# Linear attention times SwiGLU on one core: query weights prepared in other buffers, the denominators of half two placed later, phi of Q read from PSUM

## The chip, the cores and the metric

The kernel runs on one core of one Trainium2 chip. The metric is device microseconds of one execution, from the first to the last instruction of the core and what lies around them. A figure for a kernel is the median of several runs.

## The reference

The input is x, 2048 rows of 1024 in bf16. A layernorm without weights gives xn, and two branches read it.

```python
xn  = layernorm(x)                               # 2048 x 1024
q, k, v = split(xn @ wqkv)                       # 32 heads of 32
phi = lambda t: where(t > 0, t + 1, exp(t)) + 1e-6
kv  = einsum("hsd,hse->hde", phi(k), v)          # one 32 x 32 matrix a head
z   = sum of phi(k) over s
o   = (phi(q) @ kv) / (phi(q) . z + 1e-6)
s   = o @ wo
g   = silu((silu(xn @ w_gate) * (xn @ w_up)) @ w_down)    # inner width 3584
out = x + s * g
```

## The kernel before, in words

**How the work is multiplied.** Every large product is cut into pairs of output blocks, and a pair is computed with a seven-product scheme (products named 1, 2, 3, 4, 5, 6, 7 in `Pair`, L722). It needs sums and differences of the operand blocks: `WF.combos` (L639) makes four of them for a block of weights, each an instruction on 128x1024, and `WF.inner` (L648) makes those of a second level inside products 1, 5 and, for gate and up, 3. `XF.outer` and `XF.inner` do the same for the activations. `Pair` gathers the products in PSUM banks, with copies on ScalarE (ACT) and additions on VectorE (DVE), and calls `evac` for each finished quarter; a quarter comes from PSUM three times in four (`kind` is "ps") and from SBUF once (`kind` is "sb").

**Stages.** First the layernorm, the transposes and K and V: sixteen row tiles, two by two (`kv_steps`, L1156), with phi of K in `kv_out` (L1056) and the sums of phi(K) times V gathered in three banks by `a_tile`. Then the Q stage: four pairs (`q_pair`, L1271: row half p 0, 1 by weight half s 0, 1), whose `evac` calls `phi_evac` (L1035) and leaves phi(Q) in SBUF at 132 KB and above. Into it fall `kv_end` (L1200, scales the 32x32 matrices by DVE), `kvt` (their transposes on TensorE), `m_build` (L1225, sixteen products with wo that go to a scratch tensor in HBM) and `den_run(0)` (L1278, the denominators of head half one). Then 28 gate/up pairs (`gu_pair`, numbered z = 0 to 27 in the loop at L1585), the product of the normalised phi(Q) with the matrix of `m_build` (`s_pair`), and the down projection (`d_pair`). `normalise` (L1305) multiplies phi(Q) by the reciprocals, in eight calls at z = N0 to N0+7, and writes it to HBM.

**phi_evac.** ACT writes Exp of the bank to a temporary e (`H1`, one of twelve 1 KB slots); DVE does min(e, 1) + eps (L1038). With `relu` set, ACT reads the bank a second time for Relu into a second temporary and DVE adds the two (L1043, shown under L482, the line of `tt`). Otherwise one DVE instruction does max(source, 0) + e (L1045). For Q the choice is `RQ` (L312): the Relu form for quarters from PSUM. For K it is `RK` (L313): the Relu form for column block 0.

**Weights.** `wload` (L1239) takes the next number k (0, 1 are the two halves of the Q weights, 2 to 15 the gate/up blocks 0 to 13, 16 to 19 phi(Q)), loads two times 512 KB into one of three raw buffers, and plans combos and inner sums into one of three `cmb` and one of two `inn` buffers. Raw buffers are W0 (80 KB), W0+8 and R2 (198 KB). During K and V the places W0+8 to W0+28 and W0+40 to W0+44 hold sums of the K/V weights (`KC`, L957), W0+32 to W0+40 hold row tiles of x, W0+44 to W0+50 normalised rows, W0+28 to W0+32 and W0+50 to W0+52 phi(K); W0 to W0+8 and R2 are unused. The combos of Q, of gate/up block 0 (`GC0`) and all sums of activations run on DVE, the other combos and the inner sums of gate/up on GpSimd (POOL).

**What sets the order.** The code doesn't issue instructions as it goes. `Plan.op` (L77) records each operation with what it must wait for; `Plan.schedule` (L125) then plays all engines with durations of its own, lets TensorE choose within a window of 20 operations, the other engines by due time (`dl`), and fixes each engine's order; `emit` (L261) writes the waits. A load with `asap` goes as soon as its buffer is free; one without gets an extra wait on the TensorE operation that lies LEAD = 12 us ahead of its due time (L135). All DMAs go through SyncE's (SP's) queue. An operation that reads a PSUM bank is recorded as if it wrote it (L464), so readers of one bank follow one another, each with a wait, on the same engine too.

## Time and profile before

| | us |
|---|---|
| median of 5 runs | 748.19 |
| lowest, highest of them | 745.16, 751.69 |
| the profiled execution | 750.69 |
| its span on the core | 749.0 |
| TensorE busy in it | 712.6 |
| DVE, ACT, POOL busy in it | 588.6, 380.2, 261.4 |

The profiled execution is 1.69 us longer than its span, and 2.50 us longer than the median. Busy times of TensorE (PE) count pipelined matmuls, so a busy PE is not always at its full rate; idle PE time is what the views of waits name. In the trace the K/V stage ends near 113 us, the last phi of Q near 201 us, and the gate/up pairs reach from there to about 560 us.

### The profile page before, as it was taken

What the parts mean: (1) busy time and instruction counts of PE and PEld (TensorE: products, weight loads), DVE (VectorE), ACT (ScalarE), POOL (GpSimd) and SP (SyncE); (2) the same over time, 40 slices, a digit from 0 to 9 for tenths busy, and PEclk for the clock granted to TensorE, in tenths of its full rate; (3) what the DMA queues carried; (4) which work ended last, traced back from release to release, by engine and by line L of the source; (5) the groups of instructions that cost most, each with busy time, mean ns of one, the idle gap of its engine ahead of it and who ended that gap; (6) DMA issues with size and microseconds to landing.
All of it is one profiled execution on the core that took longest, in us unless ns stands there. A gap on an engine that the chain in (4) does not pass through costs nothing.

```text
span 749.0 us, 11806 instructions
## 1 busy us (share of the span) xinstructions
PE 712.6 (95%) x4247; PEld 399.6 (53%) x4247; DVE 588.6 (79%) x1127; ACT 380.2 (51%) x729; POOL 261.4 (35%) x230
## 2 busy tenths in 40 slices
PE   8998998887898899999999999999999999999996
PEld 3444444443565555556666666656554455464642
DVE  6998765999899889988888888889978965556433
ACT  4777755886646567665454454544664112121211
POOL 2011000245538547856678656712750000000000
PEclk9999999999999999999999999999999999999999
DMA  9834205131133464467322333235599257463622
GB/s 301 205 85 98 43 0 169 58 113 32 44 117 114 154 197 138 152 225 232 106 77 65 106 99 111 88 119 169 182 321 281 81 169 201 134 202 105 188 71 70
DMA packets 141978, 101.57 MB, mean 136 GB/s; under 512 B 19040, under 2 KB 137056, under 8 KB 141920
## 3 DMA queue, kind: packets, MB, share of 16 engines
q1 hardware_dynamic: 141920, 100.82, 44.8%
q8 instruction: 33, 0.54, 0.3%
q14 instruction: 25, 0.20, 0.1%
HBM read 68.16 MB, written 29.49 MB: 130 GB/s over the span
## 4 chain that ended last, share of the span: by engine, by line
PE 72%; DVE 13%; DMA 6%; ACT 5%; issue 3%; SPq 1%; DVEq 0%; ACTq 0%
PE ps L424 72%; DVE SB L482 8%; ACT SB L474 4%; DVE ps L482 1%; DMA out_dram<-SB 1%; DVE SB L1038 1%; DMA SB<-in_A_x_dram 1%; DMA SB<-SB 1%; DMA SB<-q_scratch 1%; DMA SB<-h_scratch 1%; ACT ps L474 1%; DVE SB L1045 1%; SPq L494 1%; DMA m_scratch<-SB 1%; DVE SB L1210 0%
## 5 line engine op out<-in xcount | busy, mean ns | idle before, releaser
L424 PE MATMUL ps<-SB 128*128 128x512 f16 (+4 forms) x4126 | 702.1, 331 | 24.8 <-DVE ps L482 9.0
L424 PEld LDWEIGHTS ps<-SB 128*128 128x128 f16 (+1 forms) x4126 | 393.8, 98 | 330.9 <-DVE ps L482 18.0
L482 POOL TENSOR_TENSOR SB<-SB 128x1024 f16<-128x1024 bf16 (+3 forms) x196 | 247.2, 1287 | 232.1 <-PE ps L424 112.3
L474 ACT ACTIVATE SB<-ps 128x256 f32<-128x256 f32 (+5 forms) x443 | 235.2, 566 | 143.3 <-PE ps L424 113.8
L482 DVE TENSOR_TENSOR SB<-SB 128x512 f16<-128x512 f16 (+11 forms) x360 | 238.2, 696 | 57.3 <-ACT SB L474 22.9
L482 DVE TENSOR_TENSOR SB<-ps,SB 128x256 f32<-128x256 f32 (+2 forms) x318 | 181.7, 592 | 54.8 <-PE ps L424 43.0
L482 DVE TENSOR_TENSOR ps<-ps,SB 128x512 f32<-128x512 f32 (+1 forms) x250 | 128.1, 527 | 26.0 <-PE ps L424 16.8
L474 ACT ACTIVATE ps<-ps 128x512 f32<-128x512 f32 (+1 forms) x172 | 84.4, 492 | 123.5 <-PE ps L424 91.2
L474 ACT ACTIVATE SB<-SB 128x512 f16<-128x512 f32 (+1 forms) x68 | 42.4, 624 | 88.0 <-DVE SB L482 87.9
L1002 POOL TENSOR_TENSOR rstd<-veps,neg_half 128x1 f32<-128x1 f32 x16 | 11.6, 733 | 65.1 <-DVE veps L1001 63.9
L1038 DVE TENSOR_SCALAR SB<-SB 128x512 f16<-128x512 f16 x64 | 24.4, 394 | 12.1 <-ACT SB L474 11.9
L474 ACT ACTIVATE SB<-SB,zc 128x512 bf16<-128x512 bf16 x32 | 22.3, 716 | 6.4 <-DVE SB L482 6.3
L474 ACT ACTIVATE SB<-SB,nmr,rstd 128x1024 f16<-128x1024 bf16 x12 | 14.6, 1234 | 1.1 <-DVE nmr L1004 1.1
L998 DVE BATCH_NORM_STATS2 stats<-SB 128x6 f32<-128x512 bf16 x16 | 11.0, 687 | 3.6 <-DMA SB<-in_A_x_dram 3.5
L1045 DVE SCALAR_TENSOR_TENSOR SB<-SB 128x512 bf16<-128x512 f32 x15 | 11.6, 781 | 0.1
L999 DVE BATCH_NORM_STATS2 stats<-SB 128x6 f32<-128x512 bf16 x16 | 10.9, 683 | 0.0
L424 PE MATMUL ps<-SB,ident 128*128 128x512 f16 x17 | 6.5, 557 | 1.4 <-POOL ident L505 1.4
L1045 DVE SCALAR_TENSOR_TENSOR SB<-ps,SB 128x512 bf16<-128x512 f32 x9 | 6.1, 685 | 0.0
L453 PE MATMUL ps<-ident,SB 128*128 128x128 f16 x40 | 3.1, 220 | 2.3 <-DVE SB L1210 1.4
L453 PEld LDWEIGHTS ps<-ident,SB 128*128 128x128 f16 x40 | 2.3, 98 | 4.9 <-DVE SB L1008 2.8
L424 PEld LDWEIGHTS ps<-SB,ident 128*128 128x128 f16 x17 | 2.1, 131 | 4.5 <-issue 2.8
L1295 DVE RECIPROCAL SB<-SB 128x64 f32<-128x64 f32 x8 | 4.3, 544 | 0.0
(28 smaller groups left out, 25.1 us busy)
## 6 DMA issues: line engine op xcount, KB each, us to landing
h_scratch<-SB SPq DMA_DIRECT2D x112, 128.0 KB, 2.0
SB<-h_scratch SPq DMA_DIRECT2D x16, 896.0 KB, 6.1
SB<-in_B_w_gate_dram SPq DMA_DIRECT2D x14, 512.0 KB, 4.2
SB<-in_B_w_up_dram SPq DMA_DIRECT2D x14, 512.0 KB, 5.3
SB<-in_B_w_down_dram SPq DMA_DIRECT2D x4, 1792.0 KB, 8.6
SB<-in_A_wqkv_dram SPq DMA_DIRECT2D x12, 512.0 KB, 8.4
SB<-in_A_x_dram SPq DMA_DIRECT2D x16, 256.0 KB, 4.7
SB<-r_scratch SPq DMA_DIRECT2D x32, 128.0 KB, 2.8
```

The lines of the kernel that those rows point to most:

```text
L424: last = h.matmul(o() if callable(o) else o, l() if callable(l) else l, r() if callable(r) else r, start=st, stop=sp, skip_group_check=True)
L453: last = h.transpose(o(), i(), ident[:, :])
L474: return op("act", reads, writes, lambda h: h.activation(ev(o), ev(i), func, **kw), n / 1200.0 + (0.055 if src == "ps" else 0.095) + (0.09 ...
L482: f = lambda h: h.tensor_tensor(ev(o), ev(a), ev(b), alu)
L494: f = lambda h: h.dma_start(ev(o), ev(i))
L998: dve([xr] + ([named("ve", 0)] if q == 1 else []), [sA], lambda h: h.bn_stats(stats[:, j, 0, :], xa[:, 0:512]), 512)
L999: dve([xr] + ([named("ve", 0)] if q == 1 else []), [sB], lambda h: h.bn_stats(stats[:, j, 1, :], xa[:, 512:1024]), 512)
L1002: pool([ver, nh_r], [rsr], lambda h: h.tensor_tensor(rstd[:, j, :], veps[:, j, :], neg_half[:, :], ALU.pow), 0.56)
L1038: dve([e], [e], lambda h: h.tensor_scalar(vap(e, FP16), vap(e, FP16), 1.0, EPS_PHI, ALU.min, ALU.add), 512, 3.84, urgent=PU).port = True
L1045: dve(reads + [e], [out_r], lambda h: h.scalar_tensor_tensor(out_ap, ev(src), 0.0, vap(e, FP16), ALU.max, ALU.add), 512, urgent=PU).port = ...
L1295: dve([ea], [ra], lambda h, q=q: h.reciprocal(vap(ra, F32)[:, q * 64:q * 64 + 64], vap(ea, F32)[:, q * 64:q * 64 + 64]), 400)
```

## The change

It has six parts. The raw buffers rotate in another order and from another start: Q weights half one goes to R2 and `cmb` at W0+32, half two to W0 and `cmb` at W0+16, gate/up block 0 to W0+8, block 1 to R2; from there on the rotation repeats every three blocks. The two Q loads lose `asap`; the second is due 20 us earlier (`QU`). Phi of Q always takes the L1045 form. `den_run(1)` is called at z = 2 in place of z = 0, `normalise` starts at z = 4 in place of 3, and the two early loads of down weights come at z = 13 in place of 12. A reader of a PSUM bank waits for earlier readers on other engines alone (`solo`). The buffers of the down projection (`HC`, `HT`, `H2`, `HI_AT`, `WI_AT`, the order in `cur`) move with the places that the last weight blocks leave free.

```diff
-    def op(self, eng, reads, writes, fn, busy, sem=None, ..., asap=False):
+    def op(self, eng, reads, writes, fn, busy, sem=None, ..., asap=False, solo=()):
...
+        for r in solo:
+            for k in r.keys:
+                preds.update(q for q in self.readers.get(k, ()) if q.eng != eng)
...
-                v.pool.pend.remove(o.idx)
+                v.pool.pend.remove(v.ops[0].idx)
...
-    RQ = lambda w, i, j, kind: kind == "ps"
+    RQ = lambda w, i, j, kind: False
-    N0, NA, WA = 3, 2, True
+    N0, NA, WA, QU, ZD = 4, 2, True, 20.0, 2
...
-            wr += [v.r for v in mine if v not in wv]
+            kw["solo"] = [v.r for v in mine if v not in wv]
...
-        raw_at = [W0 * KB, (W0 + 8) * KB, R2 * KB]
-        cmb_at = [(W0 + 16 + 8 * k) * KB for k in range(3)]
+        raw_at = [R2 * KB, W0 * KB, (W0 + 8) * KB]
+        cmb_at = [(W0 + 16 + 8 * k) * KB for k in (2, 0, 1)]
...
-            rk = (0, 1, 0)[k] if k < 3 else 2 - k % 3
+            rk = k % 3
...
-                        dsem("wr%d_%d_%d" % (rk, q, kts.start)), 512 * KB // len(src), asap=WA)
+                        dsem("wr%d_%d_%d" % (rk, q, kts.start)), 512 * KB // len(src), asap=WA and k > 1).urgent = QU if k == 1 else 0.0
...
-        HC = [80, 112, 199, 96, 87]
-        HT = [119, 122.5, 103, 106.5]
-        H2 = 103
+        HC = [88, 111, 199, 104, 80]
+        HT = [118, 121.5, 96.75, 100.25]
+        H2 = 96.75
...
-            if z == 0:
+            if z == ZD:
                 at.append(partial(den_run, 1))
...
-        cur, spare = [0, 2, 1, 3], 4
+        cur, spare = [0, 2, 3, 1], 4
```

## The prediction

> **What bounds the kernel now.** I read the page first, then busy time by stretch, then who TensorE (PE) waits for in the worst stretch.

> ```profile
> PE 712.6 (95%) x4247; PEld 399.6 (53%) x4247; DVE 588.6 (79%) x1127; ACT 380.2 (51%) x729; POOL 261.4 (35%) x230
> ```

> PE is the bound over the whole span, but not everywhere. Busy time by stretch (DMA share and clock at the end of each line):

> ```profile
> 80.00:100.00 20.00, 20.00 (x106) 9.51 (x105) 11.55 (x28) 14.38 (x26) 0.17 (x1) 1.00 0.14 27
> 100.00:113.00 13.00, 13.00 (x74) 6.39 (x73) 8.88 (x22) 7.61 (x15) 0.00 (x0) 1.00 0.00 0
> 113.00:203.00 90.00, 75.53 (x482) 41.07 (x484) 75.62 (x171) 64.20 (x132) 34.19 (x25) 0.98 0.28 85
> 340.00:380.00 40.00, 40.00 (x260) 25.32 (x259) 33.07 (x59) 21.30 (x43) 27.15 (x20) 1.00 0.44 138
> 177.70:181.10 3.40, 2.87 (x9) 1.31 (x10) 3.40 (x6) 1.09 (x2) 2.17 (x3) 0.50 0.00 0
> ```

> See that PE never idles at the end of K/V (80 to 113 us) and in the middle of gate/up (340 to 380), while the Q stage, 113 to 203, leaves it idle 90.00 - 75.53 = 14.5 us. DVE is as busy there as PE (75.62); ahead of it DVE is idle for 8.45 + 4.12 us. The last line is 3.4 us at half the clock. Who PE waits for from 112 to 220 us (us, times, longest):

> ```profile
> PE ps L424 <- DVE ps L482: 5.7, 4, 3.2
> PE ps L424 <- ACT ps L474: 3.1, 4, 1.0
> PE ps L424 <- ACT SB L474: 2.2, 2, 1.2
> PE ps L424 <- DVE SB L482: 1.6, 1, 1.6
> PE ps L453 <- DVE SB L1210: 1.4, 1, 1.4
> ```

> These 14.0 us are what the change can win. The longest wait, on the timeline:

> ```profile
> 170.66 5.34 DVE L1038 TENSOR_SCALAR SB<-SB 128x512 f16<-128x512 f16 x7
> 170.83 9.04 POOL L482 TENSOR_TENSOR SB<-SB 128x512 f16<-128x512 f16 x8 [0.87 <-DVE SB L482]
> 177.48 0.69 DVE L482 TENSOR_TENSOR ps<-ps,SB 128x512 f32<-128x512 f32 x1
> 178.23 3.72 PE L424 MATMUL ps<-SB 128*128 128x512 f16 x12 [3.19 <-DVE ps L482]
> ```

> Seven small DVE steps beside POOL's sums take 5.34 us, the bank addition behind them comes late, and PE idles 3.19 us. The DVE groups concerned, first in the Q stage, then in K/V (20 to 113 us), where POOL is nearly idle:

> ```profile
> L1038 DVE TENSOR_SCALAR SB<-SB 128x512 f16<-128x512 f16 x33 | 15.7, 499 | 2.8 <-ACT SB L474 2.8
> L482 DVE TENSOR_TENSOR SB<-SB 128x512 bf16<-128x512 f16 x25 | 11.4, 494 | 0.0
> L1045 DVE SCALAR_TENSOR_TENSOR SB<-SB 128x512 bf16<-128x512 f32 x8 | 6.8, 862 | 0.0
> ```

> ```profile
> L1038 DVE TENSOR_SCALAR SB<-SB 128x512 f16<-128x512 f16 x27 | 7.6, 284 | 9.2 <-ACT SB L474 9.2
> L482 DVE TENSOR_TENSOR SB<-SB 128x512 bf16<-128x512 f16 x14 | 5.6, 421 | 1.2 <-ACT SB L474 1.2
> L1045 DVE SCALAR_TENSOR_TENSOR SB<-ps,SB 128x512 bf16<-128x512 f32 x8 | 5.4, 685 | 0.0
> ```

> [...]L1038 has a mean of 499 ns beside POOL and 284 without, and additions on PSUM (128x512, one SBUF input) keep 696 and 688 ns in the Q stage. [...]the trace has 3.4 us at 0.50 right after the 3.19 us wait.[...]

> **The change part by part**, against the profiled execution of 750.69 us (span 749.0 and 1.7 around it).

> *Q weights earlier.* Half two's loads are issued at 116 and 122 us, its four combos (0.68 us each) and eight inner sums (0.29 each) follow from 126 us on DVE: 5.1 us of durations, 4.0 from start to start (instructions overlap by some 0.08). In the change they can run when K's last sums are used, by the places in the code about 105 us. Half one's, now at 107 to 113 us, can run once the last x tiles are normalised, before 90 us. That much DVE work finds 4.1 us idle in 100 to 113 and 8.45 in 80 to 100, where PE waits for nothing: I cost it at nothing. Without that cover (DVE late at the turn to Q) it costs up to 2. In the Q stage it frees DVE while `kv_end` runs: three combos (1.8 us) lie between 126.4 and 129.2, ahead of the eight L1210 steps for which the transposes wait 1.45. **-1.4**.

> *Loads.* In the trace of before, SP issues the Q half one loads at 13.0 and 14.6 us and those of gate/up block 1 at 18.0 and 24.1; these four leave the busy start (DMA share 0.94 in 0 to 20 us). PE's waits there come before 20 us and are on DVE and POOL, so nothing is won; bounds -0.5 to 0. The Q loads must instead be in time without `asap`: SP issues nothing between 84 and 113 us, so four issues of 0.4 us delay no one. Half two's leave 116 to 122, with only wo beside them.

> *Gate/up blocks 0 and 1 swap places.* Block 0 no longer waits for Q half one's raw buffer (loads at 149.6 and 156.1) but for V's sums, gone at about 125; its DVE combos (four of 0.68) and POOL's inner sums can start some 15 us earlier. Block 1 waits for Q half one instead, so POOL's four combos (2.2 us each, now 139.6 to 157.3) come after 160. POOL does the same work in another order[...]. It costs PE 1.57 us now at 158.4 (two L1038 in 2.57 us) and the 3.19 at 178.2. Bounds: both waits stay, or both go. I take half: **-0.8** and, with half of the slow clock's 3.4 x 0.5 = 1.7, **-2.4**.

> *Phi of Q.* 32 quarters, 24 from PSUM. ACT loses 24 Relu of 0.59 to 0.64 us, from start to start 0.48: 11.5 of its 64.2 us. DVE exchanges 24 additions (0.421) for 24 L1045 (0.685): 24 x 0.264 = +6.3 us. Each of the 24 also gives up one H1 slot. PE's ACT waits: 1.05 at 140.5 (ACT itself waited 1.12 for an m_scratch store to free its slot), 0.86 at 142.0, and behind both engines 0.54 at 150.9 and 1.17 at 185.2. I take nearly all of the first two and a third of the others: **-0.9, -0.7, -0.6**. DVE after: 75.6 - 4.0 + 6.3 = 77.9 us[...]. The 6.3 us lie beside PE unless DVE is last, as it is for 5.7 + 1.6 of PE's 14.0 us of waits; bounds 0 and 6.3; I take a third, **+2.1**. The bank is now held until DVE's last step, not ACT's: queued behind are the matmuls that reuse it.

> *Denominators of half two.* PE waits 1.59 us at 202.8 for the last phi before `den_run(1)`; 32 matmuls take 1.1. Two pairs later nothing waits: **-1.5**. The step's DVE part (0.42 + four of 0.54 = 2.6 us), its ACT copy and eight stores (SP, 0.6 each, 5 us) move from 204-214 to about 230. Behind them on SP stand h_scratch stores, whose slots are twelve, and loads that are early: 0, bound +1. `normalise` and two down loads come one pair (13 us) later; 203 to 350 us has the same DVE work (133 of 147), the down loads are due by their own time: 0, bounds -1 and +1.

> *solo.* Same-engine readers lose a wait. ACT's pairs are already interleaved (starts 0.27 to 0.5 us apart at 114.8 to 115.8): 0, bound -1. *Down buffers:* the same sizes in the places freed at the same times: 0, bound ±1.

> Sum: -1.4 - 0.8 - 2.4 - 0.9 - 0.7 - 0.6 + 2.1 - 1.5 = **-6.2**. Profiled: 744.5. The median of the runs shown is 2.5 below the profiled execution: 748.2 - 6.2 = **742.0**. Next late will be DVE in the Q stage.

> **Rivals.** *DVE keeps its waits (no change):* its 14.4 us of idle time in the Q stage come from the back and forth with PE, so they stay, and the stage lasts 77.9 + 14.4 = 92.3 us, +2.3; with -1.5 of the denominators +0.8: **749.0**. For it: DVE is already as busy as PE. Against: 5.3 us of the waits (3.1 + 2.2) are ACT's, and ACT is relieved. *Banks held by DVE (slower):* when DVE runs behind, as from 170.7 to 180.3, up to six banks of eight wait for L1045, which before ACT released. If PE loses 2.5 us more at each of the four turns between pairs, +10, less the kv_end, H1 and denominator gains of 3.8: +6.2, **754.4**.[...] *Nearly all waits go (more gain):* 14.0 + 1.7 less the 2.3 at 120.5, 125.3 and 195.0 us that no part touches: -13.4, **734.8**. *The Q loads come late,* since they have lost `asap`: half one's were issued 100 us ahead of their use, and LEAD is 12; a 512 KB load of wqkv takes 8.4 us (median), so they should be in time; if not, PE idles 2 to 5 us at 113 and the gain is gone: counted with no change.

> **How the numbers follow.** Forecast (-3.7 to -10) 0.58, more gain 0.12, no change 0.18, slower 0.12. Half a per cent, 3.7 us, is about what can be told from none. Faster is 0.58 + 0.12 = 0.70. The range runs from just above the large gain, 735.5, to 750, which takes in no change with its costs of +1 and leaves the slower case out; the forecast alone spans 738 to 744.5.

> **What would show it.** Right: no PE wait on L1210 near 130; combos of both Q halves before 113; block 0's POOL sums before block 1's; ACT near 52 us in the Q stage; den_run's matmuls near 230 with no wait; the stage some 6 us shorter, DVE above 90% busy. Wrong: PE waits on L1045 by name, waits for a Q load near 113, a second Exp/Silu table load, or new waits beyond 340 us.

## The result and the profile after

| | before | after |
|---|---|---|
| median, us | 748.32 (40 runs) | 744.71 (21 runs) |
| lowest, highest | 745.16, 752.60 | 742.46, 746.98 |
| profiled execution, span | 750.69, 749.0 | 742.46, 740.9 |

The ratio is 0.9947 (95%: 0.9935 to 0.9959): 3.6 us less by the medians, where 6.2 were forecast. The two profiled executions lie 8.2 us apart, because before's is one of its longer runs and after's the shortest of its 21; so the traces are used for where time went, and the medians for how much.

The page's line of engines, of after. ACT has lost the 24 Relu instructions:

```profile
PE 711.7 (96%) x4247; PEld 399.6 (54%) x4247; DVE 585.9 (79%) x1127; ACT 361.6 (49%) x705; POOL 258.4 (35%) x230
```

Busy time by stretch, with the same columns as before, for the Q stage (its window is chosen two us shorter) and for the stretch at half clock where it is now:

```profile
113.00:201.00 88.00, 79.03 (x499) 43.51 (x497) 78.30 (x172) 53.98 (x111) 34.31 (x27) 0.98 0.30 90
170.30:173.70 3.40, 3.40 (x11) 1.37 (x9) 3.40 (x4) 1.96 (x4) 3.40 (x4) 0.51 0.00 0
```

PE is now idle for 88.00 - 79.03 = 9.0 us of the stage in place of 14.5. DVE is busy for 78.30 us of 88 (the working had 77.9), ACT for 53.98 (it had 52). The last line is a warning: 3.4 us at half the clock are still there, at 170.3 instead of 177.7. The window's ends are round numbers; an event that both traces have, the table load of ACT behind its last Exp of Q, came at 187.48 us in place of 192.75, 5.3 us earlier. Who PE waits for from 112 to 220 us:

```profile
PE ps L427 <- DVE SB L485: 3.0, 1, 3.0
PE ps L427 <- ACT ps L477: 2.5, 4, 1.0
PE ps L427 <- DVE ps L485: 1.3, 2, 0.8
PE ps L427 <- DVE SB L1048: 1.1, 1, 1.1
PE ps L456 <- DVE SB L1213: 1.0, 1, 1.0
```

All in all 8.9 us against 14.0. From 220 to 360 us the waits are 6.4 against 7.1, beyond that 3.7 against 3.9. (In after, line numbers are three higher: L424 is L427, L482 is L485, L1038 is L1041, L1045 is L1048, L1210 is L1213.) The timeline of after shows which waits went and which stayed:

```profile
127.72 0.64 DVE L1048 SCALAR_TENSOR_TENSOR SB<-ps,SB 128x512 bf16<-128x512 f32 x1
128.27 2.15 DVE L1213 SCALAR_TENSOR_TENSOR SB<-ps,zinv,maskbd 128x128 f16<-128x128 f32 x8
130.48 0.62 PE L456 MATMUL ps<-ident,SB 128*128 128x128 f16 x8 [1.04 <-DVE SB L1213]
...
134.62 19.26 PE L427 MATMUL ps<-SB 128*128 128x512 f16 x110 [0.77 <-DVE ps L485]
...
159.07 16.13 POOL L485 TENSOR_TENSOR SB<-SB 128x1024 f16<-128x1024 bf16 x12 [7.89 <-DMA SB<-in_B_w_up_dram]
164.19 4.26 DVE L1041 TENSOR_SCALAR SB<-SB 128x512 f16<-128x512 f16 x3
169.71 6.39 PE L427 MATMUL ps<-SB 128*128 128x512 f16 x22 [3.01 <-DVE SB L485]
177.21 5.00 PE L427 MATMUL ps<-SB 128*128 128x256 f16 x30 [1.11 <-DVE SB L1048]
...
210.34 1.06 PE L427 MATMUL ps<-SB,Zh 128*32 128x256 bf16 x32
```

From 134.62 PE runs 110 matmuls with no wait, where before stopped twice for ACT. At 210.34 the denominators start without a wait. But at 164.19 three small DVE steps take 4.26 us, while POOL runs the sums of gate/up block 1 (16.13 us on end), and PE idles 3.01. The groups of DVE and ACT in the stage from 113 to 201 us say the same: L1041 still has a mean of 483 ns, and the fused form, with its one SBUF input, 679 (25 of them, 24 for Q):

```profile
L477 ACT ACTIVATE SB<-ps 128x512 f16<-128x512 f32 x44 | 25.6, 603 | 12.3 <-PE ps L427 12.2
L1048 DVE SCALAR_TENSOR_TENSOR SB<-ps,SB 128x512 bf16<-128x512 f32 x25 | 16.6, 679 | 0.0
L1041 DVE TENSOR_SCALAR SB<-SB 128x512 f16<-128x512 f16 x33 | 15.2, 483 | 1.7 <-ACT SB L477 1.7
```

### The profile page after: what moved, and what is told of

The parts are those of the page before. It is cut to its first block, busy times and chain, and to the rows that moved or that the text cites. A ratio compares the mean times of both kernels' runs of the same rounds, so it can differ in the third digit from the quotient of the medians.

```text
span 740.9 us, 11746 instructions
## 1 busy us (share of the span) xinstructions
PE 711.7 (96%) x4247; PEld 399.6 (54%) x4247; DVE 585.9 (79%) x1127; ACT 361.6 (49%) x705; POOL 258.4 (35%) x230
## 4 chain that ended last, share of the span: by engine, by line
PE 71%; DVE 15%; DMA 7%; issue 4%; ACT 3%; SPq 0%; DVEq 0%; ACTq 0%
PE ps L427 71%; DVE SB L485 10%; ACT SB L477 3%; DMA SB<-h_scratch 3%; DVE ps L485 2%; DMA out_dram<-SB 1%; DVE SB L1041 1%; DVE SB L1048 1%; DMA SB<-SB 1%; DMA SB<-in_A_wqkv_dram 1%; DMA SB<-q_scratch 1%; ACT ps L477 1%; DMA SB<-in_A_x_dram 0%; PE ps L456 0%; DVE SB L1213 0%
## 5 line engine op out<-in xcount | busy, mean ns | idle before, releaser
L427 PE MATMUL ps<-SB 128*128 128x512 f16 (+4 forms) x4126 | 701.4, 332 | 20.6 <-DVE SB L485 10.6
L427 PEld LDWEIGHTS ps<-SB 128*128 128x128 f16 (+1 forms) x4126 | 393.8, 98 | 325.9 <-DVE SB L485 17.8
L485 POOL TENSOR_TENSOR SB<-SB 128x1024 f16<-128x1024 bf16 (+3 forms) x196 | 244.4, 1274 | 228.2 <-PE ps L427 113.8
L477 ACT ACTIVATE SB<-ps 128x512 f32<-128x512 f32 (+4 forms) x419 | 221.9, 558 | 179.5 <-PE ps L427 164.1
L485 DVE TENSOR_TENSOR SB<-SB 128x512 f16<-128x512 f16 (+11 forms) x336 | 223.4, 700 | 57.5 <-ACT SB L477 20.3
L485 DVE TENSOR_TENSOR SB<-ps,SB 128x512 f16<-128x512 f32 (+2 forms) x318 | 180.8, 591 | 51.8 <-PE ps L427 41.4
L485 DVE TENSOR_TENSOR ps<-ps,SB 128x512 f32<-128x512 f32 (+1 forms) x250 | 128.0, 527 | 25.9 <-PE ps L427 21.1
L1005 POOL TENSOR_TENSOR rstd<-veps,neg_half 128x1 f32<-128x1 f32 x16 | 11.4, 723 | 64.4 <-DVE veps L1004 63.2
L1041 DVE TENSOR_SCALAR SB<-SB 128x512 f16<-128x512 f16 x64 | 23.8, 385 | 8.7 <-ACT SB L477 8.7
L1048 DVE SCALAR_TENSOR_TENSOR SB<-ps,SB 128x512 bf16<-128x512 f32 x33 | 22.0, 680 | 0.1
L477 ACT ACTIVATE SB<-SB,nmr,rstd 128x1024 f16<-128x1024 bf16 x12 | 14.6, 1236 | 1.2 <-DVE nmr L1007 1.1
L1048 DVE SCALAR_TENSOR_TENSOR SB<-SB 128x512 bf16<-128x512 f32 x15 | 10.3, 685 | 0.0
L427 PE MATMUL ps<-SB,ident 128*128 128x512 f16 x17 | 6.5, 555 | 1.4 <-POOL ident L508 1.4
L427 PEld LDWEIGHTS ps<-SB,ident 128*128 128x128 f16 x17 | 2.1, 131 | 4.5 <-issue 2.7
```

The costliest lines, as they stand in the source:

```text
L427: last = h.matmul(o() if callable(o) else o, l() if callable(l) else l, r() if callable(r) else r, start=st, stop=sp, skip_group_check=True)
L477: return op("act", reads, writes, lambda h: h.activation(ev(o), ev(i), func, **kw), n / 1200.0 + (0.055 if src == "ps" else 0.095) + (0.09 ...
L485: f = lambda h: h.tensor_tensor(ev(o), ev(a), ev(b), alu)
L1005: pool([ver, nh_r], [rsr], lambda h: h.tensor_tensor(rstd[:, j, :], veps[:, j, :], neg_half[:, :], ALU.pow), 0.56)
L1041: dve([e], [e], lambda h: h.tensor_scalar(vap(e, FP16), vap(e, FP16), 1.0, EPS_PHI, ALU.min, ALU.add), 512, 3.84, urgent=PU).port = True
L1048: dve(reads + [e], [out_r], lambda h: h.scalar_tensor_tensor(out_ap, ev(src), 0.0, vap(e, FP16), ALU.max, ALU.add), 512, urgent=PU).port = ...
```

## The experiments

Two theories were to be told apart. **Parts:** the gain is a sum of parts, each with its own price, as the working has it. **Coincidence:** each edit makes another plan, and the time is set by where the DVE steps that the trace of before shows held up beside POOL (L1038: a mean of 499 ns in the Q stage, 284 in K/V) fall beside POOL's long instructions (combos of 2205 ns there); then parts alone don't add up, and shorter POOL instructions help. Every kernel was timed in batches together with before. Medians in us; "beside" is before's median in the same batch.

| kernel | median | beside | ratio (95%) | difference |
|---|---|---|---|---|
| after | 744.71 | 748.32 | 0.9947 (0.9935, 0.9959) | -3.6 |
| rq_alone | 743.86 | 748.52 | 0.9937 (0.9920, 0.9955) | -4.7 |
| buf_alone | 746.08 | 748.52 | 0.9965 (0.9952, 0.9978) | -2.4 |
| den_alone | 755.14 | 748.52 | 1.0090 (1.0073, 1.0108) | +6.6 |
| solo_alone | 763.84 | 748.52 | 1.0188 (1.0166, 1.0211) | +15.3 |
| after_no_rq | 745.73 | 748.88 | 0.9961 (0.9946, 0.9977) | -3.2 |
| after_no_den | 751.31 | 748.88 | 1.0028 (1.0013, 1.0043) | +2.4 |
| after_no_solo | 748.40 | 748.88 | 0.9987 (0.9975, 1.0000) | -0.5 |
| half_combos | 739.44 | 748.88 | 0.9878 (0.9856, 0.9900) | -9.4 |
| solo_half | 753.16 | 748.46 | 1.0067 (1.0043, 1.0091) | +4.7 |
| before_half | 746.82 | 748.46 | 0.9977 (0.9966, 0.9989) | -1.6 |
| other_plan | 744.58 | 748.46 | 0.9948 (0.9933, 0.9963) | -3.9 |
| exp_on_act | 743.54 | 748.46 | 0.9931 (0.9913, 0.9950) | -4.9 |

### Parts alone, on the kernel before

**rq_alone**: phi of Q in the fused form, nothing else. (This kernel, den_alone, solo_alone and those with halves built on before also have the change's line on `pend`. It has no run of its own; by the code it removes the same entry as before's line wherever the first recorded operation on a buffer is also the first to be placed.)

```diff
-    RQ = lambda w, i, j, kind: kind == "ps"
+    RQ = lambda w, i, j, kind: False
```

> Before, with phi of Q alone in the fused form. By the prediction's terms the relief of ACT and of the H1 slots (-2.2 us) and DVE's extra 6.3 us (+2.1 on the path) cancel: 0 us, within 1. My reading after the result: the two waits for ACT near 140 us vanish and DVE isn't last there, so -1 to -2. Rival, banks held by DVE: +2 us or more, with PE waits on the fused instruction by name adding up to over 3 us.

Measured: -4.7 us alone, as much as the whole change brings (the intervals overlap). The fused form's extra DVE time is not what costs, and no stretch of the profile has a reduced clock before the last microseconds. But ACT's waits didn't go. From 112 to 220 us PE waits 5.6 us for ACT (5.4 and 0.2), where before has 5.3 (3.1 and 2.2). All waits in this stretch fell from 14.0 to 12.6 us, those from 220 us on from 11.0 to 7.5: most of the waiting that was won lies behind the stage that was edited. In the stage itself the wait ahead of the second denominators is gone, though they still stand at z = 0:

```profile
192.44 1.06 PE L424 MATMUL ps<-SB,Zh 128*32 128x256 bf16 x32
```

The fused step is due early in the plan (`PU`) and the addition of the Relu form is not, which would explain it; this was not tested apart.

**buf_alone**: the buffers and loads of the change, with the places of the down projection; that is after with three lines put back.

```diff
-    RQ = lambda w, i, j, kind: False
+    RQ = lambda w, i, j, kind: kind == "ps"
-    N0, NA, WA, QU, ZD = 4, 2, True, 20.0, 2
+    N0, NA, WA, QU, ZD = 3, 2, True, 20.0, 0
-            kw["solo"] = [v.r for v in mine if v not in wv]
+            wr += [v.r for v in mine if v not in wv]
```

> Before, with the new buffer places and the later, earlier-due Q loads alone (Q weights prepared during K/V, gate/up blocks 0 and 1 changed places, down buffers moved). By the prediction's terms -4.6 us[...]. My reading after the result: the long PE wait beside POOL stays, so -0.5 to -1.5. Rival: this part is what carries the whole gain, -3 us or more.

Measured: -2.4 us. In the one profile PE's waits from 112 to 220 us are 13.5 in place of 14.0, and from 220 to 360 us 4.9 in place of 7.1.

**den_alone**: `den_run(1)` at z = 2, `normalise` from z = 4.

```diff
-    N0, NA, WA = 3, 2, True
+    N0, NA, WA, ZD = 4, 2, True, 2
...
-            if z == 0:
+            if z == ZD:
                 at.append(partial(den_run, 1))
```

> Before, with the denominators of half two at z = 2, normalise from z = 4 and the two down loads at z = 13, nothing else. Theory: the wait of 1.6 us for the last phi ahead of the denominators goes, -1.5 us within 0.7. Rival: the matmuls behind it wait for the same late phi steps or banks, 0.

Measured: +6.6 us: slower by 0.9% (0.7 to 1.1). The two profiled executions lie only 1.7 us apart (752.44 and 750.69), so the trace shows where time went, not all of the 6.6. PE waits for DVE's additions on PSUM (L482) 9.1 us from 112 to 220 us, 5.4 of them at one time, and 9.0 us from 220 to 360, 5.2 of them at one time. The earlier one lies in phi of Q, which this edit doesn't touch. The later one on the timeline:

```profile
324.39 15.75 POOL L482 TENSOR_TENSOR SB<-SB 128x1024 f16<-128x1024 bf16 x11 [10.31 <-DMA SB<-in_B_w_up_dram]
...
330.79 8.82 DVE L482 TENSOR_TENSOR SB<-SB 128x512 f16<-128x512 bf16 x7
```

Seven steps with two SBUF inputs each (six products of `normalise` and one of gate with up) take 8.82 us beside POOL's sums of a weight block, and PE waits for the bank addition behind them, until 340.34 us. `normalise` is the step that the working moved at no cost. Within the first wait a stretch at half clock begins that lasts some 6.8 us, twice the 3.41 of those in before and after; PE works in 3.57 us of it (its line by stretch: clock 0.50):

```profile
177.50:184.30 6.80, 3.57 (x13) 1.94 (x14) 5.33 (x11) 4.02 (x9) 3.09 (x4) 0.50 0.00 0
```

**solo_alone**: readers of a bank wait only for readers on other engines.

```diff
+        for r in solo:
+            for k in r.keys:
+                preds.update(q for q in self.readers.get(k, ()) if q.eng != eng)
...
-            wr += [v.r for v in mine if v not in wv]
+            kw["solo"] = [v.r for v in mine if v not in wv]
```

> Before, where a reader of a PSUM bank waits for earlier readers on other engines alone, nothing else. Theory: 0 us within 1, the waits that go were hidden. Rival: every change of the recorded waits makes another plan, and another plan alone moves the time by 1 to 3 us either way.

Measured: +15.3 us, 1.9% slower (1.7 to 2.1). The edit only takes dependences away; what it changes is the plan. Compared in order, some 250 of the 4247 PE records of the two traces are out of line. PE's waits from 112 to 220 us total 17.2, with single ones of 4.2 and 3.6, and from 220 to 360 us there is another of 4.2. The first 4.2 is the wait for the denominators of half two:

```profile
193.50 7.53 DVE L485 TENSOR_TENSOR SB<-SB 128x512 bf16<-128x512 f16 x5
193.55 6.86 POOL L485 TENSOR_TENSOR SB<-SB 128x1024 f16<-128x1024 bf16 x3 [13.23 <-DMA SB<-in_B_w_up_dram]
...
201.08 1.90 PE L427 MATMUL ps<-SB,Zh 128*32 128x256 bf16 x32 [4.24 <-DVE SB L485]
```

Five additions of the Relu form, two SBUF inputs each, take 7.53 us beside POOL's combos. The whole change has neither these additions nor denominators at this place, so this cost of solo can't arise there. The profile has five stretches at reduced clock before the end, where before's has two. The sum of the four parts alone is -4.7 - 2.4 + 6.6 + 15.3 = **+14.8**; together they give **-3.6**. The theory of parts falls here.

### After, less one part

**after_no_rq**, **after_no_den** and **after_no_solo** each put back one line of before:

```diff
+    RQ = lambda w, i, j, kind: kind == "ps"
```

> After, with phi of Q from PSUM in the Relu form again. Theory, the fused phi carries the gain (alone it gave -4.7 us): at least 2 us slower than after, 747 us or more, with PE waits on ACT back in the Q stage. Rival, the parts don't add up and any plan will do: within 1.5 us of after's 744.7, or faster.

Measured: 1.0 us worse than after by the medians, with intervals that overlap. Alone the fused form was worth 4.7, here about 1. Here it does relieve ACT: PE's waits for ACT from 112 to 220 us are 7.0 us without it and 2.5 with it. But this profile has no stretch at half clock before its end, where after's has two.

```diff
+    N0, NA, WA, QU, ZD = 3, 2, True, 20.0, 0
```

> After, with the denominators of half two at z = 0, normalise from z = 3 and the down loads at z = 12 again. Theory of the prediction (1.5 us won where nothing waits for the denominators): 746 us. Rival, what this part moves is where normalise meets GpSimd's sums: it can go either way by several us, as it did alone (+6.6).

Measured: 6.6 us worse than after. The same edit that costs 6.6 us on before is worth 6.6 us here. The wait that it was meant for is only 0.3 of this: the denominators of half two, back at z = 0, start at 187.90 us after PE has waited 0.30. The longest wait is 4.46 us, at 279 us, behind six steps with two SBUF inputs (five products of `normalise`, one of gate with up) that take 6.45 us beside POOL's combos.

```diff
+            wr += [v.r for v in mine if v not in wv]
```

> After, where every reader of a bank follows the readers before it again. Theory, solo has no cost or gain of its own and its +15.3 us alone came of the plan that it made: 744.7 us within 3, either way. Rival, solo is slow in itself[...]: some 10 us faster than after.

Measured: 3.7 us worse than after, though solo alone cost 15.3. The longest wait is 4.30 us, at 332 us, and again behind a row of steps with two SBUF inputs: seven of them take 7.88 us beside POOL's combos. No part that was put in alone and also left out has the same worth in both places; the buffers were not left out.

### Shorter instructions on GpSimd

**half_combos**: after, with each of POOL's combos (128x1024) as two of 128x512. The work is the same.

```diff
-                    tt([a[1], b[1]], [o[1]], o[0], a[0], b[0], alu, 1024, True, eng[n])
+                    if eng[n] == "pool":
+                        for w in range(2):
+                            tt([a[1], b[1]], [self.cmb_r((0, 1, 2, 3)[n], w)],
+                               o[0][:, w], a[0][:, w], b[0][:, w], alu, 512, True, "pool")
+                    else:
+                        tt([a[1], b[1]], [o[1]], o[0], a[0], b[0], alu, 1024, True, eng[n])
```

> After, with each of GpSimd's combos of 128x1024 as two instructions of 128x512, same work. Theory, [...]the 3.0 us PE wait near 170 us (three small DVE steps in 4.26 us beside four combos) shrinks to under 2 and no slow clock follows it: -1 to -3 us against after, plan permitting. Rival, DVE's own amount of work is the limit: the wait stays within 0.5 us of 3.0, and the time is after's or some us more because GpSimd has 48 more instructions.

Measured: 739.44 us, 5.3 below after and 9.4 below before (ratio to before 0.9878, 0.9856 to 0.9900): the fastest kernel here. A POOL combo now takes 1205 ns in the Q stage in place of 2153. But the wait of the Q stage for which the halves were made didn't shrink. PE's waits of half_combos, first from 112 to 220 us, then from 220 to 360:

```profile
PE ps L427 <- DVE SB L485: 4.7, 2, 3.9
```

```profile
PE ps L427 <- DVE SB L485: 2.3, 5, 0.8
```

and of after, from 220 to 360 us:

```profile
PE ps L427 <- DVE SB L485: 5.1, 4, 2.6
```

The longest wait of the Q stage went from 3.0 to 3.9 us. From 220 to 360 us the longest went from 2.6 to 0.8, the total from 6.4 to 3.9, and the stretch at half clock that after has at 276 us is gone. In after that wait stood behind this pair, two products of `normalise` in 4.43 us beside combos:

```profile
265.13 9.35 POOL L485 TENSOR_TENSOR SB<-SB 128x1024 f16<-128x1024 bf16 x5 [7.19 <-DMA SB<-in_B_w_up_dram]
...
269.53 4.43 DVE L485 TENSOR_TENSOR SB<-SB 128x512 f16<-128x512 bf16 x2
...
274.95 6.40 PE L427 MATMUL ps<-SB 128*128 128x256 f16 x29 [2.63 <-DVE SB L485]
```

So the gain fits the theory, but its place was another than expected: in the gate/up stage, not around phi of Q. What the halves do to one held-up step shows in the small steps of the Q stage (shortest, median and longest in ns), first in after, then in half_combos:

```profile
L1041 DVE TENSOR_SCALAR SB<-SB x33: 229/289/2201, 113.3 to 187.0; 128x512 f16<-128x512 f16 x33
L1045 DVE TENSOR_SCALAR SB<-SB x32: 273/282/1242, 122.9 to 187.1; 128x512 f16<-128x512 f16 x32
```

The longest went from 2.20 to 1.24 us, each time about one POOL instruction (2.15 and 1.21 us), so no small step waited through two halves. The mean stayed (483 and 499 ns), because more of the steps were held up (5 took over 1 us, in place of 3). How much of the 5.3 us is owed to this isn't shown: the halves make another plan too, and from 220 to 360 us the 32 products of `normalise` take 21.4 us in place of 22.9.

**solo_half**: solo_alone with the same halves (the two diffs together).

```diff
+            kw["solo"] = [v.r for v in mine if v not in wv]
...
+                        for w in range(2):
```

> The kernel with solo alone (763.8 us), with GpSimd's combos in halves of 128x512, same work. Theory, its loss is small DVE steps that wait behind GpSimd's long instructions, then PE, then the slow clock: at least 6 us of the 15 come back, 758 or less. Rival, the loss lies in the order itself[...]: less than 2 us come back.

Measured: 10.7 of solo_alone's 15.3 us come back. The dependences are solo_alone's, so this much of its loss was no fixed price of the dependences. With halves in both kernels solo costs 753.16 - 746.82 = 6.3 us (before_half follows), without them 15.3.

**before_half**: before with the halves alone.

```diff
+                        for w in range(2):
```

> Before, with GpSimd's combos in halves of 128x512 and nothing of the change. Theory, [...]about the 5 us that the halves gave on after, 743 to 746. Rival, the halves only suit after's plan: within 1.5 us of before, or slower.

Measured: -1.6 us. Some 5 us were expected, as on after: a miss. In its profile the waits after 220 us fell from 11.0 to 7.3 (3.8 up to 360 us, 3.5 beyond), as they did in half_combos, but those of the Q stage rose from 14.0 to 16.0, and three stretches at half clock stand where before has two. A price of the halves that is the same in every plan doesn't exist either.

### Two more changes of the plan

**other_plan**: after with another urgency of phi in the planner (`PU`), which moves some instructions (some 100 of the 4247 PE records of the two traces are out of line) and changes no work.

```diff
-    UBANK, PU = 0.0, 6.0
+    UBANK, PU = 0.0, 3.0
```

> After, with the phi steps due 3 us ahead in place of 6 in the planner's list: the same instructions, waits and data, another order. Theory, the parts don't add up because each makes another plan and the chip doesn't follow the planner's clock: moves by 1 to 6 us either way from after's 744.7. Rival, plans are equal when the work is, and the parts' own costs explain their times: within 0.7 us.

Measured: 744.58, the same as after. It was expected to move by 1 to 6 us: a miss. Another order need not be another time.

**exp_on_act**: after, with DVE's small step (a mean of 483 ns in after's Q stage) taken out for the 24 quarters from PSUM. ACT computes Relu of minus the bank, then Exp of minus that; DVE does max(bank, eps) + e in one instruction. It leaves out the 1e-6 for positive t.

```diff
+                act(reads, [e], partial(vap, e, FP16), src, ACT.Relu, 512, kind, scale=-1.0)
+                act([e], [e], partial(vap, e, FP16), partial(vap, e, FP16), ACT.Exp, 512, "sb", scale=-1.0)
+                dve(reads + [e], [out_r], lambda h: h.scalar_tensor_tensor(
+                    out_ap, ev(src), EPS_PHI, vap(e, FP16), ALU.max, ALU.add), 512, urgent=PU).port = kind == "sb"
```

> After, with phi of the 24 Q quarters from PSUM without its small DVE step: ACT does Relu(-t) and Exp of its negative, DVE max(t, eps) + e, [...]and ACT has 24 instructions more (+11.5 us, in a stage where it is busy 54 of 88 us). Theory, [...]the 3.0 us wait near 170 us and the slow clock behind it go, -2 to -5 us against after. Rival, ACT becomes the last (two steps in a row before DVE's): PE waits for ACT instead, 0 to +4.

Measured: 743.54 (738.26 to 748.67), 1.2 below after by the medians and within the spread of runs. PE's longest wait in the Q stage is 2.7 us, and it is for the fused step itself (L1043). The stage's waits fall from 8.9 to 7.5 us, but those from 220 to 360 us rise from 6.4 to 8.6 and those beyond from 3.7 to 6.0, and the half-clock stretches stay at two. What is won at one place is again paid back at another.

## Why the prediction was right or wrong

The sign held, and the range held the time; 744.7 lies just beyond the forecast's own span, which ended at 744.5. By steps, with PE's waits in the two traces:

| step | worked out | in the traces |
|---|---|---|
| transposes behind `kv_end` | -1.4 | 1.45 to 1.04: -0.4 |
| wait beside POOL at 158.4 | -0.8 | 1.57 to none: -1.6 |
| wait beside POOL at 178.2, with the clock | -2.4 | 3.19 to 3.01, clock loss unchanged: -0.2 |
| ACT at 140.5 and 142.0 | -0.9, -0.7 | 1.05 and 0.86 to none: -1.9 |
| 150.9 and 185.2 | -0.6 | 0.54 and 1.17 to 0.93 (at 154.8): -0.8 |
| DVE time of the fused form | +2.1 | new waits 0.77 (134.6) and 1.11 (177.2): +1.9 |
| denominators | -1.5 | 1.59 to none: -1.6 |
| table load near 195 us | untouched | 1.0 to 0.24: -0.8 |

The lines add to -5.4; the view of waits gives 8.9 - 14.0 = -5.1 for the stage.

**Right, with limits.** Against the waits of these two traces, ACT, the denominators and the price of the fused form were sized nearly as measured. For ACT the reason given holds inside the change: its 24 instructions are gone (68 to 44 in the group), and without the fused form PE waits 7.0 us for ACT in place of 2.5. On the kernel before it did not hold (rq_alone: 5.6, before: 5.3). The denominators' wait went, but moving them was not what it took: with the fused form they wait 0.30 us at z = 0 in after_no_den and not at all in rq_alone. They also came at 210 us, not near 230. PE did wait for the fused step by name, which the prediction had called a sign of being wrong, but for 1.1 us at one turn; the rival with 2.5 us at all four turns didn't come: the fused form keeps 679 ns in the Q stage, with POOL busy for 34.31 us of the 88, against 685 in K/V of before.

**The `kv_end` term was mis-sized** (-1.4 for -0.4). The combos did leave: those of Q half two are done before 116 us. But DVE filled the freed time with a combo of gate/up block 0 (at 125.97), which the change itself makes possible so early, another sum (127.00) and the L1048 step at 127.72, all ahead of the eight L1213. Freed time on a busy engine went to whatever was next in its order.

**The term of POOL's order failed in part.** The step was that POOL's work in another order would remove about half of the two waits beside it (1.57 and 3.19 us) and half of the slow clock; that half was the author's estimate. One of the two waits went. The other stays, because block 1's four combos and inner sums, which the change itself moves behind 159 us, now lie where DVE does phi: POOL 16.13 us on end from 159.07. The clock's share was not won at all: the two profiles both have two stretches of 3.4 us at half clock before the end. In the waits the term came to -1.8 us in place of -3.2.

**"Moved at no cost" failed as a way of reasoning.** The working priced solo at 0 (bound -1), the shift of `normalise` and the down loads at 0 (bounds -1 and +1). Alone solo came to +15.3; the denominators with this shift, priced at -1.5 in all, came to +6.6. Inside the whole change leaving either out makes it slower, by 3.7 and 6.6, but no view of before's profile could tell that. Where these losses show, one form comes back: in den_alone, after_no_den and after_no_solo the longest wait of the gate/up stage (5.2, 4.5 and 4.3 us) stands behind a row of six or seven steps with two SBUF inputs, `normalise`'s for the most part, beside POOL's combos. That parts don't add up is shown by the experiments. That the range held nevertheless is in part luck: the four parts, each priced by its own run, add to +14.8.

**Lost clock is part of it, but a smaller part than the mean clock suggests.** The clock's loss by (1 - mean clock) times the run has a mean of 9.4 us in den_alone and 11.4 in solo_alone, against 4.0 in before. This counts half clock in which PE has nothing to do. In den_alone's profile it gives 8.3 us, but before PE's last matmul there are 13.7 us at half clock and PE works in 8.0 of them, which by the clock of 0.50 costs at most 4.0, an estimate; in before's it works in 6.3, at most 3.1.

**Left open.** From 112 us on, the waits of the two traces differ by 25.0 - 19.0 = 6.0 us, the executions themselves by 8.2 and the medians by 3.6; the 2.6 us between forecast and median can't be shared out among the terms by two single traces. Which coincidence costs what in each plan was not settled: no kernel with the order held fixed and one overlap alone removed was made. Why the halves bring 5.3 us on after and 1.6 on before isn't settled either, and other_plan shows that a small reorder can be worth nothing.

## What to carry to other kernels

Where a planner fixes the order, price an edit by the plan that it gives, not by the instructions that it touches: a dependence removed or a step moved two pairs can cost or win several times what the trace shows at its own place (here +15.3 us against a price of 0, +6.6 against -1.5). Where a trace shows VectorE steps that take longer beside a row of long GpSimd instructions (here a small `TENSOR_SCALAR` with a mean of 499 ns in place of 284, and seven steps with two SBUF inputs in 8.82 us), try shorter GpSimd instructions, and look for the gain over the whole span, since it may come elsewhere than at the wait that suggested it (here -5.3 us on after, -1.6 on before). Look at the granted clock beside each long TensorE wait (here 3.4 us at 0.50 came with waits of 2.20 and 3.19 us in before), and count a lower clock only where TensorE works.

## What the runs showed of the hardware that was not expected

**Half clock came with some PE waits of 2 to 4 us and not with others.** In these traces 3.4 us at half clock came with waits of 3.19 and 2.20 us in before, 3.01 and 2.63 in after, 3.9 in half_combos, and 6.8 us with each of the waits of 5.4 and 5.2 in den_alone. None came with waits of 2.2 and 2.1 us in rq_alone (clock 1.00 from 113 to 350 us) and 2.5 in after_no_rq (its mean clock is 0.998), and none with 3.03 us in den_alone. In before the stretch with the wait of 3.19 us begins at 177.66 us, not after the wait but while PE still waits (until 178.23). So the length of the wait alone doesn't decide.

```profile
256.17:259.58 3.41, 1.21 (x7) 0.51 (x6) 3.41 (x5) 1.24 (x3) 2.63 (x3) 1.00 0.34 135
259.58:262.99 3.41, 3.41 (x15) 1.86 (x13) 2.55 (x6) 0.30 (x1) 1.31 (x2) 0.50 0.27 96
```

```profile
310.60:314.01 3.41, 1.78 (x11) 1.01 (x12) 3.41 (x7) 2.15 (x5) 3.33 (x4) 1.00 0.38 154
314.01:317.43 3.42, 3.42 (x24) 2.10 (x22) 3.34 (x8) 2.12 (x5) 0.06 (x1) 1.00 0.38 112
```

With pieces of 3.413 us laid out from these starts, up to PE's last matmuls, PE is idle for 2.62 and 2.20 us in two pieces of before and for 2.78 and 2.21 in two of after, and each of the four is followed by one at half clock. In all the others PE is idle for at most 1.55 us (before) and 1.07 (after), and none of them is followed by half clock. (The ends of matmuls are modelled, so these figures are rough.) Whether a limit lies between 1.63 and 2.20 us, or whether there is one at all, isn't shown by these three. Before's mean clock ranges from 0.990 to 0.999 over its runs, so one plan doesn't lose the same in each execution. At a clock of 0.50 a stretch of 3.41 us costs at most half its length, 1.7 us by estimate, and less where PE is idle in it.

**What a POOL instruction costs one DVE step.** A `TENSOR_SCALAR` on 128x512 has a mean of 284 ns in K/V of before, where POOL is nearly idle, and in after the three at 164.19 take 4.26 us beside POOL's sums; two products of `normalise` took 4.43 us beside POOL's combos of 2.1 to 2.2 us. The longest single small step of the Q stage took 2.20 us in before and in after, and 1.24 us in half_combos, where a combo's half takes 1.2: in these three traces the longest one is close to one whole GpSimd instruction.
